# Gate logits of a windowed-attention and Sinkhorn-MoE kernel, with the attention output as the stationary operand

## The chip, the cores and the metric

The kernel runs on one core of a Trainium2 chip. The metric is the device time of the whole kernel in microseconds (us): the median over runs on the chip. One further execution of the same program was recorded by the hardware profiler, and all rows below are from that one.

## What is computed

A sliding-window attention over 2304 tokens (4 sequences of 576, 8 heads of 64), whose output `x` (2304 x 512) goes into a mixture of 8 experts. The weights of the experts come from gate logits `x @ w_gate` (2304 x 8), turned into shares by eight rounds of row and column scaling:

```python
attn = softmax(mask(scale * q @ k.T))       # window of 64, causal
x = (attn @ v).transpose(0, 2, 1, 3).reshape(B * S, H * D)

logits = x @ w_gate                          # N x 8
logits = logits - logits.max()
P = np.exp(logits)
for _ in range(8):
    P /= P.sum(1, keepdims=True) + 1e-09
    P /= P.sum(0, keepdims=True) + 1e-09
    P *= N / E
for e in range(E):
    out += P[:, e:e + 1] * (np.maximum(x @ w1[e], 0.0) @ w2[e])
```

All operands are float32.

## The kernel before, in words

The tokens are 18 tiles of 128 (`T` is 18); the 512 features are `KD` = 4 blocks of 128. The kernel has two stages.

The first, some 196 us, is the loop over `s` (line 622). Step `s` loads a later tile, makes the scores of tile `s` (`products`, matmuls on line 415), transposes the next tile's keys and queries (`transposes`, line 395), transposes the softmax of tile `s - 1` (`attn_T`, line 469) and multiplies it by the values (`values`, line 484). The result stands in PSUM with the features on the partitions and the tokens along the free dimension. ScalarE rounds it to fp32r (the type that TensorE multiplies in a single pass) into `xs[j][:, 0]` (line 490), VectorE puts the remainder into `xs[j][:, 1]` (line 491), and ScalarE copies the plain float32 into `xr[j]` (line 494). A pair of tiles shares one `j`. A product of such split operands is three matmuls: high by high, high by low, low by high.

Between these, `do_fill` takes the first half of expert 0 from a list: `mm1_s` (line 569, hidden layer of one pair of tiles, 12 matmuls of 256 columns) and `mm2_s` (line 583, output of one tile, 12 matmuls of 512 columns). Every even step from 4 on also calls `gate(j)` right after the scores, and `gate_T(j)` near its end. After the loop (lines 722 to 731) come the last gate, the rest of the list and the maximum of all logits.

`gate` multiplies in plain float32: for each feature block, the gate weights `wg` (128 x 32, of which 8 columns are used and the rest are zero) are the stationary operand and 256 columns of `xr` move (line 526). Each of the four blocks writes 32 partitions of its own in one PSUM tile. ScalarE copies that tile to `gt` (line 528). `gate_T` turns `gt` back with two transposes (line 535), and VectorE adds the four blocks into `logit` (line 536). In the profile a plain float32 matmul shows as two matmul records, so the four of a gate are `x8` there.

The second stage is the remaining seven and a half experts, three passes over six tiles each, in Strassen-like products (line 217, line 276, line 1194). It uses `logit` through `prob`, at its start.

The order on each engine is the order of the calls in the code (`tc.manual_schedule()`): each engine works through its queue in that order. PSUM tiles named `hp` and `yp` come from one pool of three buffers (line 327), handed out in turn.

Of the kernel before, what the change touches and what calls it, by code (L numbers as in the profile page):

```python
# [8 lines left out]
F32 = mybir.dt.float32  # L9
F32R = mybir.dt.float32r  # L10
AF = mybir.ActivationFunctionType
ALU = mybir.AluOpType
AX = mybir.AxisListType
# [8 lines left out]
def window_attention_sinkhorn_moe(ctx: ExitStack, tc: tile.TileContext, q, k, v, w_gate, w1, w2, out):  # L22
    nc = tc.nc
    B, H, S, D = q.shape
    NT, DM = out.shape
    E, _, FF = w1.shape
    P = 128
    WIN = 64
    T = NT // P
    KD = DM // P  # L30
# [20 lines left out]
    ident = const.tile([P, P], F32, name="ident")  # L51
    make_identity(nc, ident)
    logit = const.tile([P, T, E], F32, name="logit")
# [22 lines left out]
    def f32(ap):  # L76
        return ap.bitcast(F32)
# [126 lines left out]
    ps = {}  # L204
# [104 lines left out]
    qT, kT, s_t, r_t, nm_t, sum_t, aT, xr = {}, {}, {}, {}, {}, {}, {}, {}  # L309
# [13 lines left out]
    with tc.manual_schedule():  # L323
        with ExitStack() as p1:
            at_p = p1.enter_context(tc.tile_pool(name="at", bufs=2))
# [24 lines left out]
                    return masks["bot"]  # L350
                return masks["mid"]

            wg = at_p.tile([P, KD, 32], F32, name="wg", tag="wg", bufs=1)
            nc.vector.memset(wg, 0.0)

            def load_v(t):
                x = at_p.tile([P, H, D], F32, tag="v", name="v", bufs=3)
                for o, n, bb, s in runs(t):
                    nc.sync.dma_start(out=x[o:o + n], in_=v[bb, :, s:s + n, :].rearrange("h p d -> p h d"))
                raw["v", t] = x  # L360

            def load_kq(t, parts=((0, H),)):
                x = at_r.tile([P, 2, H, D], F32, tag="kq", name="kq")
                raw["kq", t] = x
                for h0, h1 in parts:
                    for i, src in enumerate((k, q)):
                        for o, n, bb, s in runs(t):
                            nc.sync.dma_start(out=x[o:o + n, i, h0:h1], in_=src[bb, h0:h1, s:s + n, :].rearrange("h p d -> p h d"))

            def load_vs(t):  # L370
                x = at_p.tile([P, H, D], F32, tag="vs", name="vs")
                if t == 0:
                    nc.vector.memset(x[0:WIN], 0.0)
                else:
                    nc.sync.dma_start(out=x[0:WIN], in_=raw["v", t - 1][WIN:P])
                nc.sync.dma_start(out=x[WIN:P], in_=raw["v", t][0:WIN])
                raw["vs", t] = x
# [143 lines left out]

            def gate(j):

                gp = ps["h"]()
                for kk in range(KD):
                    nc.tensor.matmul(gp[32 * kk:32 * kk + 32, :2 * P], lhsT=wg[:, kk, :], rhs=xr[j][:, kk, :], start=True, stop=True)
                gt = at_p.tile([P, 2 * P], F32, tag="gt", name="gt", bufs=1)
                nc.scalar.copy(out=gt, in_=gp[:, :2 * P])
                state_g[j] = gt

            def gate_T(j):
                gt = state_g.pop(j)
                gq = ps["h"]()[:, :2 * P].rearrange("p (t c) -> p t c", t=2)
                for i in range(2):
                    nc.tensor.transpose(gq[:, i, :], gt[:, i * P:(i + 1) * P], ident)
                nc.vector.tensor_reduce(
                    out=logit[:, 2 * j:2 * j + 2, :], in_=gq.rearrange("p t (a c) -> p t c a", a=4)[:, :, 0:E, :], axis=AX.X, op=ALU.add)

            later = []
            state_g = {}  # L540
            xs = {}


# [4 lines left out]
            def fetch_s(kind, c):  # L548
                if kind == "w1":
                    stg = r_stg.new()  # L550
                    nc.sync.dma_start(out=stg, in_=w1[0, :, c * P:(c + 2) * P].rearrange("(k p) f -> p k f", p=P))
                    return [stg[:, :, 0:P], stg[:, :, P:2 * P]]

                stg = acc[:, c:c + 2, :]
                nc.sync.dma_start(out=stg, in_=w2[0, c * P:(c + 2) * P, :].rearrange("(c p) d -> p c d", p=P))
                return [stg[:, 0, :], stg[:, 1, :]]
# [65 lines left out]
            for s in range(T + 1):  # L622
                if s + 2 < T and s != 3:
                    load_kq(s + 2)
                if s == 1:
                    held.append(fetch_s("w1", 2))
                if s < T:
                    load_vs(s)
                if s + 1 < T:
                    load_v(s + 1)  # L630
                if s == 3:
                    x_parts(0)
                if s == 0:
                    held.append(fetch_s("w1", 0))
                if s == 1:
                    nc.sync.dma_start(out=wg[:, :, 0:E], in_=w_gate.rearrange("(k p) e -> p k e", p=P))
                if s == 2:
                    held.append(fetch_s("w2", 0))
                    load_kq(5)
                    held.append(fetch_s("w2", 2))  # L640
                joint = 2 <= s < T
                ahead = s in (1, 2)
                if s < T:
                    products(s, (0, 1) if joint else (0,))
                    masked(s, 0)
                if s >= 4 and s % 2 == 0:
                    gate((s - 4) // 2)
                if s < 2:
                    keep_clock(4 if s else 0)
                if s == 3:  # L650
                    keep_clock(4, ps["h"]()[:, :P])
                    do_fill(1)
                if s + 1 < T:
                    transposes(s + 1)
                if s == 1:
                    keep_clock(2)
                if s < T and not ahead:
                    exps(s, 0)
                if joint:
                    masked(s, 1)  # L660
                if later:
                    later.pop(0)()
                if s != 3:
                    do_fill(1)
                if 0 <= s - 1 < T:
                    attn_T(s - 1, 0)
                if s < 2:
                    products(s, (1,))
                    masked(s, 1)
                if ahead:  # L670
                    if s == 2:
                        keep_clock(11, ps["h"]()[:, :P])
                    attn_T(s - 1, 1)
                    exps(s, 0)
                if s < T:
                    normalise(s, 0)
                if s == 0:
                    keep_clock(4)
                if 0 <= s - 1 < T and not ahead:
                    attn_T(s - 1, 1)  # L680
                if s > 2:
                    warm_weights(s)
                if s == 2:
                    values(1, lambda: exps(2, 1))
                elif s < T:
                    exps(s, 1)
                if later:
                    later.pop(0)()
                do_fill(1 if s < T else 0)
                if s == 3:  # L690
                    warm_weights(s)
                if s >= 4 and s % 2 == 0:
                    gate_T((s - 4) // 2)
                if s == 1:
                    keep_clock(4)
                if 0 <= s - 1 < T:
                    if s != 2:
                        values(s - 1)
                    raw.pop(("v", s - 2), None)
                if s < T:  # L700
                    normalise(s, 1)
                if s < 3:
                    warm_weights(s)
                if s >= 2 and s % 2 == 0:
                    j = s // 2 - 1
                    if j:
                        x_parts(j)
                    for c in range(4):
                        fill.append((0.5, lambda c=c, j=j: mm1_s(j, c)))
                    for t in (2 * j, 2 * j + 1):  # L710
                        fill.append((1, lambda t=t: mm2_s(t)))
                if s == T - 4:
                    fetch1(0)
                    sums1(0)
                if s == T - 3:
                    split1(0)
                    fetch1(1)
                    fetch2(0)
                if s == T - 1:
                    sums1(1)  # L720

            do_fill(0.5)
            gate(T // 2 - 1)
            do_fill(1)
            gate_T(T // 2 - 1)
            nc.vector.tensor_reduce(out=max1, in_=logit, axis=AX.XY, op=ALU.max)
            do_fill(1)
            mp = ps["h"]()[0:1, :P]
# [61 lines left out]
        with ExitStack() as p2:  # L790
# [85 lines left out]
            for u in range(n_units):  # L876
                s = 2 * u
# [98 lines left out]
        with ExitStack() as p3:  # L976
# [352 lines left out]
            for p, F, S, flow in plans:  # L1329
# [24 lines left out]
                for i in range(1, n):  # L1354
                    e = groups[i][0]
# [14 lines left out]
                a, b = S[-1][1], S[-1][0]  # L1370
# [112 lines left out]
```

## Time and profile before

| what | us |
|---|---|
| median of 3 runs | 1555.45 |
| lowest and highest run | 1554.54, 1555.67 |
| profiled execution, first to last instruction (span) | 1553.7 |
| TensorE matmul busy | 1546.4 |
| TensorE weight load busy | 1476.7 |
| VectorE busy | 965.2 |
| ScalarE busy | 761.3 |
| GpSimd busy | 990.6 |

The profiled execution has no device time of its own beside its span; the median of the runs is 1.75 us above that span, which is the launch and end around the first and last instruction. PE is the matmul part of TensorE and PEld its weight loads, which overlap the matmuls. Matmuls are pipelined, so the duration of one is longer than the distance from one to the next; what a stretch of matmuls costs is read from the chain of waits, where pieces follow each other without overlap.

### The profile page before, as it was taken

The page shows a single profiled execution, that of the slowest core. Times are in us where ns is not written, and L with a number is a line of the kernel's source. Part 1 is how long each engine was busy: PE and PEld are TensorE (multiplying, and loading weights), DVE is VectorE, ACT ScalarE, POOL GpSimd, SP SyncE. Part 2 cuts the span into 40 slices and gives each one's busy share as a digit, 9 for nine tenths or more (in the row PEclk, how much of TensorE's full clock was granted, in tenths as well). Part 3 has the DMA queues.
Part 4 walks back from the last instruction along what each step waited for, and adds up shares of the span by engine and source line. Part 5 has one row for each costly group of instructions (what it writes and reads, how often), then busy time and mean ns, then how long its engine had stood idle before and what let it go on. Part 6 is the DMA issues. An engine that isn't in the chain of part 4 may idle for free.

```text
span 1553.7 us, 27222 instructions
## 1 busy us (share of the span) xinstructions
PE 1546.4 (100%) x9703; PEld 1476.7 (95%) x9703; DVE 965.2 (62%) x1794; ACT 761.3 (49%) x1677; POOL 990.6 (64%) x925
## 2 busy tenths in 40 slices
PE   9999999999999999999999999999999999999998
PEld 8888889989998899899999999999999999999998
DVE  6766566665555555665665665665755675666666
ACT  6666535443443344355555554544554544554552
POOL 6244467668767776356677677566676566567565
PEclk9999999999999999999999999999999999999999
DMA  9876467557766766796766766655975665665643
GB/s 214 226 168 148 132 235 285 204 191 270 270 232 238 253 224 211 272 352 195 244 205 217 248 207 196 221 180 182 355 253 179 203 209 174 207 210 171 204 158 102
DMA packets 239876, 335.70 MB, mean 216 GB/s; under 512 B 71122, under 2 KB 154174, under 8 KB 235774
## 3 DMA queue, kind: packets, MB, share of 16 engines
q1 hardware_dynamic: 239742, 333.97, 66.6%
q8 instruction: 77, 1.26, 0.3%
q14 instruction: 57, 0.47, 0.1%
HBM read 236.34 MB, written 90.63 MB: 210 GB/s over the span
## 4 chain that ended last, share of the span: by engine, by line
PE 97%; DMA 1%; POOL 1%; DVE 1%; ACT 0%; SPq 0%; issue 0%; POOLq 0%; DVEq 0%; ACTq 0%
PE qb L217 18%; PE y L276 15%; PE qa L217 12%; PE qb L1194 12%; PE qc L217 12%; PE qa L1194 8%; PE qc L1194 8%; PE yp L583 3%; PE hp L569 3%; PE vp L484 1%; PE sp L415 1%; PE tp L469 1%; PE tp L395 1%; DMA acc<-in_moe_w_dram 1%; POOL w1c L164 0%; DMA kq<-in_q_dram 0%
## 5 line engine op out<-in xcount | busy, mean ns | idle before, releaser
L217 PE MATMUL qb<-xc,w1c 128*128 128x384 f32 x1620 | 321.2, 336 | 0.0
L1081 POOL TENSOR_TENSOR G<-sm,G 128x384 fp32r<-128x384 f32 x176 | 178.9, 1016 | 197.4 <-ACT G L1077 195.5
L217 PEld LDWEIGHTS qb<-xc,w1c 128*128 128x128 f32 x1620 | 284.9, 188 | 0.8 <-ACT qb L1095 0.3
L276 PE MATMUL y<-w2c,g 128*128 128x512 f32 x1080 | 251.3, 391 | 0.1
L276 PEld LDWEIGHTS y<-w2c,g 128*128 128x128 f32 x1080 | 201.8, 188 | 42.3 <-DVE acc L295 0.5
L217 PE MATMUL qa<-xc,w1c 128*128 128x384 f32 x1080 | 213.4, 337 | 0.0
L217 PE MATMUL qc<-xc,w1c 128*128 128x384 f32 x1080 | 213.0, 336 | 0.0
L217 PEld LDWEIGHTS qa<-xc,w1c 128*128 128x128 f32 x1080 | 190.4, 188 | 1.2
L217 PEld LDWEIGHTS qc<-xc,w1c 128*128 128x128 f32 x1080 | 190.1, 188 | 0.0
L1202 DVE TENSOR_TENSOR acc<-qb,acc 128x384 f32<-128x384 f32 x171 | 95.1, 556 | 123.3 <-PE qb L1194 110.7
L774 POOL TENSOR_TENSOR w2c<-wr,w2c 128x512 fp32r<-128x512 f32 x99 | 126.2, 1293 | 32.9 <-ACT w2c L773 31.6
L774 POOL TENSOR_TENSOR wp<-wr,wp 128x512 fp32r<-128x512 f32 x100 | 127.7, 1294 | 26.8 <-ACT wp L773 23.9
L178 POOL TENSOR_TENSOR w2c<-stg,w2c 128x512 fp32r<-128x512 f32 x60 | 83.8, 1417 | 93.8 <-PE qb L217 81.7
L1077 ACT CAST G<-sm 128x384 fp32r<-128x384 f32 x180 | 92.3, 514 | 64.3 <-DVE sm L1088 64.3
L1194 PE MATMUL qb<-G,w2c 128*128 128x384 f32 x552 | 111.2, 336 | 0.0
L1194 PE MATMUL qb<-G,wp 128*128 128x384 f32 x528 | 106.2, 336 | 0.0
L1194 PEld LDWEIGHTS qb<-G,w2c 128*128 128x128 f32 x552 | 97.7, 188 | 0.0
L295 DVE SCALAR_TENSOR_TENSOR acc<-y,prob,acc 128x512 f32<-128x512 f32 x72 | 54.0, 750 | 69.4 <-PE y L276 68.8
L1194 PEld LDWEIGHTS qb<-G,wp 128*128 128x128 f32 x528 | 93.4, 188 | 0.0
L1202 DVE TENSOR_TENSOR acc<-qc,acc 128x384 f32<-128x384 f32 x116 | 64.4, 555 | 41.3 <-PE qc L1194 40.6
L463 POOL TENSOR_TENSOR s<-s,rr 128x512 f32<-128x512 f32 x36 | 37.5, 1041 | 77.1 <-DVE rr L462 66.9
L162 ACT CAST w1c<-ws 128x1024 fp32r<-128x1024 f32 x30 | 31.6, 1054 | 99.4 <-POOL ws L147 99.4
(214 smaller groups left out, 2950.6 us busy)
## 6 DMA issues: line engine op xcount, KB each, us to landing
w1c<-w1d SPq DMA_DIRECT2D x300, 256.0 KB, 4.6
w1d<-w1c SPq DMA_DIRECT2D x30, 1792.0 KB, 7.8
stg<-in_moe_w_dram SPq DMA_DIRECT2D x66, 512.0 KB, 3.9
w1c<-w1d SPq DMA_DIRECT2D x60, 512.0 KB, 5.0
wr<-w2d SPq DMA_DIRECT2D x114, 256.0 KB, 3.6
wr<-in_moe_w_dram SPq DMA_DIRECT2D x85, 256.0 KB, 3.8
w2d<-tf SPq DMA_DIRECT2D x30, 512.0 KB, 4.8
vs<-v SPq DMA_DIRECT2D x35, 128.0 KB, 4.4
```

The source lines that it names most:

```text
L178: nc.gpsimd.tensor_tensor(out=w[:, 1], in0=src[:, j], in1=f32(w[:, 0]), op=ALU.subtract)
L217: nc.tensor.matmul(bank, lhsT=w[:, ws, a, kk, :], rhs=xc[xs][:, b, kk, :], start=(first and j == 0), stop=(j == 5), skip_group_check=not f ...
L276: nc.tensor.matmul(yp, lhsT=g[:, a, o:o + P], rhs=w[:, x, :], start=(i == 0), stop=(i == 11))
L295: nc.vector.scalar_tensor_tensor(out=at, in0=yp, scalar=pr, in1=at, op0=ALU.mult, op1=ALU.add)
L463: nc.gpsimd.tensor_tensor(out=st, in0=st, in1=rr[:, :, None].to_broadcast([P, 4, P]), op=ALU.mult)
L569: nc.tensor.matmul(hp, lhsT=w1s[c][:, a, kk, :], rhs=xs[j][:, b, kk, :], start=(i == 0), stop=(i == 3 * KD - 1))
L583: nc.tensor.matmul(yp, lhsT=g[:, a, o * P:(o + 1) * P], rhs=w[:, x, :], start=(i == 0), stop=(i == 11))
L774: nc.gpsimd.tensor_tensor(out=t[:, :, 1, :], in0=r, in1=f32(t[:, :, 0, :]), op=ALU.subtract)
L1077: nc.scalar.copy(out=self.g[:, k, 0, :], in_=src)
L1081: eng.tensor_tensor(out=self.g[:, k, 1, :], in0=src, in1=f32(self.g[:, k, 0, :]), op=ALU.subtract)
L1194: nc.tensor.matmul(bank, lhsT=W[p, u, wp][:, g, y, cols], rhs=G7[p, 2 * u + g][:, gp, x, :], start=(start and j == 0), stop=(j == 5), skip ...
L1202: nc.vector.tensor_tensor(out=at, in0=src, in1=at, op=ALU.add)
```

## The change

The gate's operands change places. The stationary operand is now a 128 x 128 block of `xs`, high or low part, and the moving operand is a new tile `wgs` that holds the split gate weights: for the high part of `x`, 16 columns of high and low weights, for the low part the high weights and 8 zero columns. The logits of 128 tokens come out with the tokens on the partitions, so there is no copy to `gt`, no transpose back, and one PSUM tile less per gate. VectorE adds the two halves. `wgs` is made once, at step 3, by two ScalarE casts and one GpSimd subtraction. `xr` stays: lines 503 to 512 use it.

```diff
-            wg = at_p.tile([P, KD, 32], F32, name="wg", tag="wg", bufs=1)
-            nc.vector.memset(wg, 0.0)
+            wg = at_p.tile([P, KD, E], F32, name="wg", tag="wg", bufs=1)
+            wgs = at_p.tile([P, KD, 2, 2, E], F32R, name="wgs", tag="wgs", bufs=1)
+            nc.vector.memset(f32(wgs), 0.0)
...
             def gate(j):
 
-                gp = ps["h"]()
-                for kk in range(KD):
-                    nc.tensor.matmul(gp[32 * kk:32 * kk + 32, :2 * P], lhsT=wg[:, kk, :], rhs=xr[j][:, kk, :], start=True, stop=True)
-                gt = at_p.tile([P, 2 * P], F32, tag="gt", name="gt", bufs=1)
-                nc.scalar.copy(out=gt, in_=gp[:, :2 * P])
-                state_g[j] = gt
-
-            def gate_T(j):
-                gt = state_g.pop(j)
-                gq = ps["h"]()[:, :2 * P].rearrange("p (t c) -> p t c", t=2)
+                gp = ps["h"]()[:, :4 * E].rearrange("p (t a c) -> p t a c", t=2, a=2)
                 for i in range(2):
-                    nc.tensor.transpose(gq[:, i, :], gt[:, i * P:(i + 1) * P], ident)
-                nc.vector.tensor_reduce(
-                    out=logit[:, 2 * j:2 * j + 2, :], in_=gq.rearrange("p t (a c) -> p t c a", a=4)[:, :, 0:E, :], axis=AX.X, op=ALU.add)
+                    for kk in range(KD):
+                        for a in range(2):
+                            nc.tensor.matmul(gp[:, i], lhsT=xs[j][:, a, kk, i * P:(i + 1) * P], rhs=wgs[:, kk, a], start=(kk + a == 0), stop=(kk == KD - 1 and a == 1))
+                nc.vector.tensor_reduce(out=logit[:, 2 * j:2 * j + 2, :], in_=gp.rearrange("p t a c -> p t c a"), axis=AX.X, op=ALU.add)
...
                 if s == 1:
-                    nc.sync.dma_start(out=wg[:, :, 0:E], in_=w_gate.rearrange("(k p) e -> p k e", p=P))
+                    nc.sync.dma_start(out=wg, in_=w_gate.rearrange("(k p) e -> p k e", p=P))
+                if s == 3:
+                    for a in range(2):
+                        nc.scalar.copy(out=wgs[:, :, a, 0], in_=wg)
+                    nc.gpsimd.tensor_tensor(out=wgs[:, :, 0, 1], in0=wg, in1=f32(wgs[:, :, 0, 0]), op=ALU.subtract)
...
-                if s >= 4 and s % 2 == 0:
-                    gate_T((s - 4) // 2)
...
-            gate_T(T // 2 - 1)
```

The order on TensorE in step 6, before, from the scores to the values (rows left out are the other `yp` products of the same two tiles):

```order
L415 MATMUL sp<-kT,qT 64x128 x16
L526 MATMUL hp<-xr,wg 32x256 x4
L395 MATMUL tp<-ident,kq 128x128 x8
L583 MATMUL yp<-w2c_232,g_0_991 128x512 x3
...
L535 MATMUL hp<-ident,gt 128x128 x2
L484 MATMUL vp<-aT,vs 64x64 x4
```

and in the changed kernel, where the same calls have other line numbers (415 is 416, 395 is 396, 583 is 575, 484 is 485):

```order
L416 MATMUL sp<-kT,qT 64x128 x16
L529 MATMUL hp<-wgs,xs 128x16 x16
L396 MATMUL tp<-ident,kq 128x128 x8
L575 MATMUL yp<-w2c_233,g_0_1002 128x512 x3
L575 MATMUL yp<-w2c_234,g_1_1018 128x512 x3
```

The gate keeps its place and has 16 matmuls instead of 4; the two transposes ahead of the values are gone.

The order on VectorE in the same step, before:

```order
L436 TENSOR_TENSOR s<-sp,mask_mid 128x512
L441 TENSOR_REDUCE nm<-s 128x4
L397 COPY kT<-tp 128x4x128
...
L462 RECIPROCAL rr<-rr 128x4
L536 TENSOR_REDUCE logit<-hp 128x16
L491 TENSOR_TENSOR xs<-vp,xs 128x4x128
```

and in the changed kernel:

```order
L437 TENSOR_TENSOR s<-sp,mask_mid 128x512
L442 TENSOR_REDUCE nm<-s 128x4
L530 TENSOR_REDUCE logit<-hp 128x16
L398 COPY kT<-tp 128x4x128
...
L463 RECIPROCAL rr<-rr 128x4
L492 TENSOR_TENSOR xs<-vp,xs 128x4x128
```

The sum into `logit` moves from the end of the step to a place ahead of the copy of the transposed keys.

The order on ScalarE at step 3, in the changed kernel:

```order
L553 CAST w1s_231<-stg_353 128x512
L553 CAST w1s_232<-stg_353 128x512
L631 CAST wgs<-wg 128x4x8 x2
L564 ACTIVATE g_0_648<-hp 128x256
```

The two casts of the gate weights are new there, between the casts of line 561 and the first activation of line 572 before.

## Rows read from the trace of the kernel before

**Rows 1.** The page: busy time of the engines, chain that ended last.

```profile
PE 1546.4 (100%) x9703; PEld 1476.7 (95%) x9703; DVE 965.2 (62%) x1794; ACT 761.3 (49%) x1677; POOL 990.6 (64%) x925
...
PE 97%; DMA 1%; POOL 1%; DVE 1%; ACT 0%; SPq 0%; issue 0%; POOLq 0%; DVEq 0%; ACTq 0%
```

**Rows 2.** Windows, core 0: us, busy of PE, PEld, DVE, ACT, POOL, PEclk, DMA.

```profile
54.00:160.00 106.00, 106.00 (x1303) 93.43 (x1303) 71.62 (x155) 69.81 (x195) 47.62 (x61) 1.00 0.72 169
```

**Rows 3.** Chain of waits in order of time, two steps: start us, us, what.

```profile
55.54 1.03 PE sp L415 x32
56.58 0.57 PE hp L526 x8
57.15 1.02 PE tp L395 x8
...
60.91 0.87 PE tp L469 x8
61.79 2.77 PE yp L583 x12
64.56 0.22 PE hp L535 x2
...
66.89 1.02 PE tp L395 x8
67.91 2.85 PE hp L569 x24
...
200.28 1.04 PE qa L217 x6
```

**Rows 4.** Weight loads by shape, 0 to 200 us: busy, mean ns | idle before.

```profile
L569 PEld LDWEIGHTS hp<-xs,w1s 128*128 128x128 f32 x432 | 52.5, 188 | 0.9 <-issue 0.6 <-DVE xs L491 0.3
...
L469 PEld LDWEIGHTS tp<-ident,s 128*128 128x128 f32 x144 | 16.5, 141 | 1.7 <-POOL s L463 0.4 <-issue 0.2
...
L526 PEld LDWEIGHTS hp<-xr,wg 128*32 128x32 f32 x72 | 1.4, 108 | 1.6 <-issue 1.6
...
L729 PEld LDWEIGHTS hp<-ident,max 128*1 128x1 f32 x1 | 0.1, 82 | 0.0
```

**Rows 5.** Timeline of weight loads, 195.8 to 197.3: start us, us, what [idle before].

```profile
196.23 0.29 PEld L817 LDWEIGHTS qc<-max,ones 1*128 1x128 f32 x2 [0.35 <-issue]
196.54 0.30 PEld L849 LDWEIGHTS qb<-xc 128*128 128x128 f32 x2
```

**Rows 6.** Timeline of PE after the first gate.

```profile
37.35 3.15 PE L583 MATMUL yp<-w2c,g 128*128 128x512 f32 x12
...
41.14 0.66 PE L469 MATMUL tp<-ident,s 128*128 128x128 f32 x4 [0.19 <-POOL s L463]
41.55 2.99 PE L583 MATMUL yp<-w2c,g 128*128 128x512 f32 x12
```

**Rows 7.** Chain of waits around the last two gates.

```profile
175.76 2.98 PE yp L583 x12
...
179.26 0.59 ACT aT L471
...
184.02 0.57 PE hp L526 x8
184.59 3.05 PE hp L569 x24
...
187.86 2.84 PE hp L569 x24
```

**Rows 8.** Timeline of ScalarE at step 3.

```profile
29.33 0.39 ACT L572 ACTIVATE g<-hp 128x256 fp32r<-128x256 f32 x1 [1.04 <-PE hp L569]
```

**Rows 9.** Timeline of VectorE in step 6.

```profile
64.81 0.23 DVE L536 TENSOR_REDUCE logit<-hp 128x16 f32<-128x64 f32 x1 [2.65 <-PE hp L535]
```

**Rows 10.** Timeline of PE: matmuls on a tile of ones, the first ones and later ones.

```profile
1.03 3.78 PE L617 MATMUL idle<-ones 128*128 128x128 f32 x16 [1.03 <-DVE ones L50]
...
19.78 2.62 PE L617 MATMUL hp<-ones 128*128 128x128 f32 x22
```

More of the change, by code (lines that the diff above doesn't have):

```diff
@@ L522, in gate @@
             def gate(j):
-                gp = ps["h"]()
-                for kk in range(KD):
-                    nc.tensor.matmul(gp[32 * kk:32 * kk + 32, :2 * P], lhsT=wg[:, kk, :], rhs=xr[j][:, kk, :], start=True, stop=True)
-                gt = at_p.tile([P, 2 * P], F32, tag="gt", name="gt", bufs=1)
-                nc.scalar.copy(out=gt, in_=gp[:, :2 * P])
-                state_g[j] = gt
-            def gate_T(j):
-                gt = state_g.pop(j)
-                gq = ps["h"]()[:, :2 * P].rearrange("p (t c) -> p t c", t=2)
+                gp = ps["h"]()[:, :4 * E].rearrange("p (t a c) -> p t a c", t=2, a=2)
                 for i in range(2):
-                    nc.tensor.transpose(gq[:, i, :], gt[:, i * P:(i + 1) * P], ident)
-                nc.vector.tensor_reduce(
-                    out=logit[:, 2 * j:2 * j + 2, :], in_=gq.rearrange("p t (a c) -> p t c a", a=4)[:, :, 0:E, :], axis=AX.X, op=ALU.add)
+                    for kk in range(KD):
+                        for a in range(2):
+                            nc.tensor.matmul(gp[:, i], lhsT=xs[j][:, a, kk, i * P:(i + 1) * P], rhs=wgs[:, kk, a], start=(kk + a == 0), stop=(kk == KD - 1 and a == 1))
+                nc.vector.tensor_reduce(out=logit[:, 2 * j:2 * j + 2, :], in_=gp.rearrange("p t a c -> p t c a"), axis=AX.X, op=ALU.add)
             later = []
-            state_g = {}
             xs = {}
```

## The prediction

> **What bounds the kernel now.** I read the page first: TensorE's matmul row is busy through the whole span, and the chain of work that ended last runs 97% through it [rows 1]. A kernel that is TensorE's from end to end still has stretches with other limits, so I read the stretch that the change touches. In the windows, TensorE has not one idle slice between 54 and 160 us, while VectorE, ScalarE and GpSimd are busy for 72, 70 and 48 us of those 106 [rows 2]. The chain in order of time then gives the price of each piece there: it goes from one TensorE piece to the next, with nothing of another engine between [rows 3]. So in this stage a microsecond added to TensorE's queue is a microsecond of kernel time, and a microsecond taken from another engine is worth nothing. Two places differ. After the first gate TensorE waits for GpSimd [rows 6], and around the last two gates the chain passes through ScalarE's copy of the transposed softmax [rows 7].
>
> **What the change removes.** Per gate, 0.57 us in the chain for the four matmuls on `wg` (eight records), the same at 56.58 and at 184.02 [rows 3, 7]. They are cheap for their columns because each of the four fills only 32 columns of the array and the four run side by side. The two transposes of `gate_T` cost 0.22 us [rows 3]. Eight of the nine lie in the chain. The eighth call, in the last step, lies in the wait for ScalarE's copy at 179.26 [rows 7] and saves nothing. Removed: 9 x 0.57 = 5.13 us and 8 x 0.22 = 1.76 us.
>
> ScalarE's nine copies to `gt` and VectorE's wait of 2.65 us for the transposes [rows 9] go too. Both are off the path, and I price them at nothing: the cover is TensorE itself, which waits for neither engine between 54 and 160 us [rows 2].
>
> **What it adds.** Per gate 16 matmuls (two tiles, four feature blocks, two parts), each with its own 128 x 128 stationary block in fp32r and 16 columns moving. No row of before has this form, so I bound it. Two things could set the pace: the columns that move or the weights that load.
>
> By columns: fp32r matmuls of 256, 384 and 512 columns follow each other in 2.85 / 24 = 0.119, 1.04 / 6 = 0.173 and 2.77 / 12 = 0.231 us [rows 3]. That is 0.44 ns a column, so 16 columns would take 0.119 - 240 x 0.00044 = 0.014 us, and 16 of them 0.22 us.
>
> By weights: loads of 1, 32 and 128 columns last 82, 108 and 188 ns [rows 4]. That is a fixed 82 ns, under which the next load can already run, and 106 ns that grow with the columns, 0.83 ns each. The pairs in the timeline say the same: two loads of 188 ns take 0.30 us together, so the second starts 0.11 us after the first [rows 5]. In the long products this is hidden, since a load of 0.11 us fits under a matmul of 0.119 us or more [rows 3]. With 16 columns moving there is nothing left to hide it under. I take **0.11 us** a matmul, the row nearest in kind: 16 x 0.11 = 1.76 us a gate, against 0.57. The least the loads allow is 0.106 and the most, if the 256-column pace is itself that of its loads, 0.119.
>
> Nine gates: 9 x (1.76 - 0.57) = **+10.71 us**. From this come off:
> - the transposes, **-1.76 us**;
> - the wait after the first gate. From 37.35 to 41.55 the queue takes 4.20 us for one set of 12 products and eight transposes, which elsewhere take 2.77 + 0.87 = 3.64 us [rows 3, 6]. The 0.56 us between are waits for GpSimd's weights and its softmax, and a later gate fills them: **-0.56 us**;
> - the change of array shape. Work on the full array that follows small tiles starts late: eight transposes take 1.02 us after the scores or the narrow gate, 0.87 us after full-size work [rows 3]. With a full-size gate this is paid by the gate and no longer by the transposes behind it, net zero. Only the last gate has full-size work on both sides, and there 3.05 - 2.85 = 0.20 us vanish [rows 3, 7]: **-0.20 us**.
>
> Sum: 10.71 - 1.76 - 0.56 - 0.20 = **+8.2 us**, with +7.6 at 0.106 and +9.5 at 0.119 us a matmul.
>
> The small edits go together. The two casts and the subtraction on 128 x 32 elements at step 3 are bounded by nothing below and 0.39 us each above, the row of an eight times larger activation beside them [rows 8]. ScalarE waits 1.04 us for TensorE right behind them [rows 8], and whatever reached TensorE would end in the 0.56 us counted above. The sum into `logit` now stands ahead of the copy of the keys on VectorE, 0.23 us [rows 9]. The scores of the next step need that copy, but a whole step later. One PSUM tile less per gate only loosens the rotation of three. `xs` is finished before `xr`, so the gate waits for nothing new.
>
> The profiled execution has a span of 1553.7 us and would go to 1561.9; the median of the runs stands 1.75 us above that span, so the forecast for the median is 1555.45 + 8.2 = **1563.6 us**.
>
> **Rivals.** Slower or faster here means by over 0.2% (3.1 us), about what a measurement of this kernel can tell from no change.
>
> *Columns set the pace.* If the weight loads kept ahead of the short matmuls, a gate would be 0.22 us: 9 x (0.22 - 0.57) - 1.76 - 0.20 = -5.1 us, **1550.3 us**, faster. It decides as soon as loads follow each other in under some 0.04 us. For it speaks that TensorE fetches weights ahead; against it, that even loads without a wait between them start 0.11 us apart [rows 5]. The Trainium skill, page "TensorE: Matmul & The Clock Gate", section "Back-to-back issue gap", gives about 25 ns from start to start for 1 to 64 moving columns; by that the gate would take 0.4 us and the kernel an estimated 1552.0 us, and no row of before has so few columns in a run to test it. Chance 6%.
>
> *Loads at the speed of the transposes.* The float32 transposes load 128 columns in 141 ns [rows 4], 59 above the fixed 82. If fp32r blocks taken from `xs` loaded like that, the gate would be 16 x 0.059 = 0.94 us, the first one hidden whole: 8 x 0.37 - 1.76 - 0.20 = +1.0 us, **1556.5 us**, no change that can be told. Against it: all fp32r loads of 128 columns here last 188 ns, the 432 of the hidden layer as an example [rows 4]. The Trainium skill, the page "TensorE: Matmul & The Clock Gate" again, section "Weight-path perf modes", says that a fast load turns itself on for 128 weights unless the type is FP32, at about twice the speed; by that the gate would be an estimated 0.85 us and the kernel about the time of before, and the 188 ns row says that fp32r does not get it. Chance 8%.
>
> *Load and matmul in series.* If a load could not run under so short a matmul, each pair would cost more. The one pair with a tiny moving operand, one column, takes 196.54 - 196.23 = 0.31 us for two, 0.155 each [rows 5]: 9 x (2.48 - 0.57) - 2.52 = +14.7 us, **1570.1 us**. With no overlap at all, 0.188 + 0.014 = 0.20 us, it would be +21.4 us, 1576.9 us. Against it: loads of 188 ns starting 0.11 us apart do overlap [rows 5]. Chance 14%.
>
> *The clock falls.* Its granted level is 1.00, 2.4 GHz, through the stage [rows 2], and a gate is now 1.8 us of little arithmetic between scores and transposes. At the start, where TensorE had done nothing, matmuls on ones took 3.78 / 16 = 0.236 us, later 2.62 / 22 = 0.119 us [rows 10]. If each gate brought the lower level, 1.2 GHz, for the 1.02 + 2.77 us behind it, nine gates would cost 34 us more, some **1598 us**. Against it: scores, narrow gate and transposes in a row did not lower it. Chance 4%.
>
> **How the numbers follow.** The forecast, loads in a row at 0.106 to 0.119 us, gets the remaining 68%. Faster: 6%, the columns. No change: 8%, the fast loads. Slower: 68 + 14 + 4 = 86%. The range takes the forecast, the fast loads and the lower half of the series case, 68 + 8 + 7 = 83%: **1556 to 1570 us**.
>
> **What would show it.** In the chain after, the gate should be a piece of 16 matmuls of about 1.9 us (1.76 and 0.15 for the change of shape), the transposes behind it 0.87 instead of 1.02 us, and the two steps from scores to scores 1.0 us longer. The weight loads of the gate should last 188 ns and start 0.11 us apart. PEclk should stay 1.00. A gate of under 1 us, or a wait of TensorE for another engine inside the stage, would make the prediction wrong.

## The result and the profile after

| what | before | after |
|---|---|---|
| median of 5 runs each on one chip, us | 1555.21 | 1564.93 |
| lowest and highest run, us | 1554.54, 1555.67 | 1564.61, 1565.89 |
| profiled span, us | 1553.7 | 1563.9 |
| first stage, to the first matmul of `qb<-xc`, us | 196.5 | 204.6 |
| second stage, from there to the end, us | 1357.2 | 1359.3 |

The ratio is 1.0063 with a 95% interval of 1.0052 to 1.0075: the changed kernel is slower by 9.7 us, where 8.2 were forecast. The profiled execution of the changed kernel is the slowest of its five runs (spans 1562.6 to 1563.9 us).

The page of the changed kernel: TensorE has 54 more matmul records, and the chain that ended last, 97% TensorE before [rows 1], now has 2% of GpSimd.

```profile
PE 1555.1 (99%) x9757; PEld 1489.0 (95%) x9757; DVE 964.9 (62%) x1794; ACT 758.7 (49%) x1670; POOL 991.8 (63%) x926
...
PE 94%; POOL 2%; DMA 1%; DVE 1%; ACT 1%; issue 0%; SPq 0%; POOLq 0%; DVEq 0%; ACTq 0%
```

The windows of the stretch that [rows 2] show for before: TensorE is still never idle, at a granted clock of 1.00, and the other three engines have slack as before.

```profile
54.00:162.00 108.00, 108.00 (x1312) 98.00 (x1311) 68.06 (x149) 64.93 (x184) 44.73 (x58) 1.00 0.68 159
```

The chain in order of time, at the places of [rows 3] and [rows 7]:

```profile
55.65 1.03 PE sp L416 x32
56.68 1.88 PE hp L529 x16
58.56 0.95 PE tp L396 x8
59.51 2.76 PE yp L575 x12
...
77.69 1.88 PE hp L529 x16
...
191.25 1.69 PE hp L529 x16
192.94 5.79 PE hp L561 x48
```

The gate has gone from 0.57 to 1.88 us, the piece of `gate_T` (0.22) is gone, and from one gate to the next pass 77.69 - 56.68 = 21.01 us. Before, the same period was 76.60 - 56.58 = 20.02 us, with the first of them in [rows 3] and the second here:

```profile
76.60 0.57 PE hp L526 x8
```

The weight loads, as groups by shape over the first stage, and then the timeline of one gate:

```profile
L561 PEld LDWEIGHTS hp<-xs,w1s 128*128 128x128 f32 x432 | 52.4, 188 | 0.4 <-DVE xs L492 0.3 <-issue 0.2
L529 PEld LDWEIGHTS hp<-wgs,xs 128*128 128x128 f32 x144 | 16.8, 191 | 1.4 <-issue 1.2
```

```profile
56.61 1.86 PEld L529 LDWEIGHTS hp<-wgs,xs 128*128 128x128 f32 x16 [0.17 <-issue]
```

Sixteen loads of 0.19 us each take 1.86 us from the first start to the last end, so they start (1.86 - 0.19) / 15 = 0.111 us apart.

After the first gate, the timeline of TensorE no longer shows the waits of [rows 6]; from one set of products to the next pass 41.88 - 38.25 = 3.63 us, where it was 4.20:

```profile
38.25 3.00 PE L575 MATMUL yp<-w2c,g 128*128 128x512 f32 x12
41.09 1.04 PE L470 MATMUL tp<-ident,s 128*128 128x128 f32 x8
41.88 1.39 PE L575 MATMUL yp<-w2c,g 128*128 128x512 f32 x5
```

So far this is the prediction: the first stage is 8.0 us longer (204.56 against 196.54). Some 2 us of the profiled execution are in the second stage, which the change does not touch. There the waits of TensorE between 190 and 560 us, none before, now have one line:

```profile
PE qb L217 <- ACT qb L237: 1.6, 2, 1.4
```

I followed it back through the changed kernel. ScalarE's timeline:

```profile
365.61 1.04 ACT L162 CAST w1c<-ws 128x1024 fp32r<-128x1024 f32 x1 [8.43 <-POOL ws L147]
366.56 0.47 ACT L237 COPY qb<-qa 128x384 f32<-128x384 f32 x1
```

GpSimd's timeline:

```profile
349.00 0.74 POOL L302 TENSOR_TENSOR xt<-tf 128x256 f32<-128x256 f32 x1 [8.16 <-DVE g L227]
...
364.78 0.80 POOL L147 TENSOR_TENSOR ws<-stg,ws 128x256 f32<-128x256 f32 x1
```

The timeline of SP's queue:

```profile
338.86 0.34 SPq L855 DMA_DIRECT2D tf<-xd_f  x1
```

Read from the bottom: SP issues a load of `xd_f` (activations of a later pass) at 338.86, GpSimd uses it at 349.00, 10.14 us later. (The view puts GpSimd's wait down to VectorE's `g`, which ended last, at 348.98; the load itself landed 10.0 us after its issue, so it was late by itself. In the second profile of this kernel, below, the wait is put down to the load.) Behind it GpSimd's queue holds the weight sums up to line 147, ScalarE's cast waits for them until 365.61, and the copy on line 237, for which TensorE waits, stands behind that cast. In the kernel before, the same load was used 338.76 - 330.88 = 7.88 us after its issue, and the copy waited for TensorE and not the other way round. SP's queue, before:

```profile
330.88 0.33 SPq L862 DMA_DIRECT2D tf<-xd_f  x1
```

GpSimd, before:

```profile
338.76 0.78 POOL L302 TENSOR_TENSOR xt<-tf 128x256 f32<-128x256 f32 x1 [5.90 <-DMA tf<-xd_f]
```

ScalarE, before:

```profile
355.20 1.05 ACT L162 CAST w1c<-ws 128x1024 fp32r<-128x1024 f32 x1 [8.44 <-POOL ws L147]
356.74 0.46 ACT L237 COPY qb<-qa 128x384 f32<-128x384 f32 x1 [0.48 <-PE qa L217]
```

The experiments ask two things: what makes a gate 1.88 us, and where the second stage's time comes from.

### The profile page after: what moved, and what is told of

Same layout as the page of the kernel before. It is cut to its first block, busy times and chain, and to the rows that moved or that the text cites. A ratio compares the mean times of both kernels' runs of the same rounds, so it can differ in the third digit from the quotient of the medians.

```text
span 1563.9 us, 27327 instructions
## 1 busy us (share of the span) xinstructions
PE 1555.1 (99%) x9757; PEld 1489.0 (95%) x9757; DVE 964.9 (62%) x1794; ACT 758.7 (49%) x1670; POOL 991.8 (63%) x926
## 3 DMA queue, kind: packets, MB, share of 16 engines
q8 instruction: 77, 1.26, 0.4%
## 4 chain that ended last, share of the span: by engine, by line
PE 94%; POOL 2%; DMA 1%; DVE 1%; ACT 1%; issue 0%; SPq 0%; POOLq 0%; DVEq 0%; ACTq 0%
PE qb L217 17%; PE y L276 13%; PE qb L1187 12%; PE qa L217 12%; PE qc L217 12%; PE qa L1187 8%; PE qc L1187 8%; PE hp L561 3%; PE yp L575 3%; PE vp L485 1%; PE hp L529 1%; PE sp L416 1%; PE tp L470 1%; POOL w1c L164 1%; PE tp L396 1%; DMA tf<-xd_f 1%
```

## Experiments on the gate

**128 columns moving (cols128).** The changed kernel with 112 columns of zeros beside the 16.

```diff
-            wgs = at_p.tile([P, KD, 2, 2, E], F32R, name="wgs", tag="wgs", bufs=1)
+            wgs = at_p.tile([P, KD, 2, 16, E], F32R, name="wgs", tag="wgs", bufs=1)
...
```

> The changed kernel with 128 columns moving in each gate matmul instead of 16 (the 112 more are zeros); everything else the same. If the weight load sets the pace, a gate stays at 16 matmuls in 1.88 us in the chain, starts 0.107 us apart, and the first stage ends (first matmul of line 842 before the second stage) within 0.3 us of the changed kernel's 204.6 us. If the moving columns set the pace, at 0.44 ns a column, each matmul grows by 0.049 us, a gate by 0.79 us to 2.7 us, and the stage ends near 211.7 us.

Measured: one run of 1564.4 us, and in the chain

```profile
56.66 1.93 PE hp L529 x16
58.59 0.89 PE tp L396 x8
```

Eight times the columns add 0.05 us to a gate of 16 matmuls, and the transposes behind it take 0.06 less. The columns do not set the pace.

**Half the stationary block (half_load).** The changed kernel with 64 instead of 128 tokens in each stationary block; it leaves out the logits of the other 64.

```diff
-                            nc.tensor.matmul(gp[:, i], lhsT=xs[j][:, a, kk, i * P:(i + 1) * P], rhs=wgs[:, kk, a], start=(kk + a == 0), stop=(kk == KD - 1 and a == 1))
+                            nc.tensor.matmul(gp[0:64, i], lhsT=xs[j][:, a, kk, i * P:i * P + 64], rhs=wgs[:, kk, a], start=(kk + a == 0), stop=(kk == KD - 1 and a == 1))
...
```

> The changed kernel with 64 instead of 128 columns in each gate's stationary operand: the gate logits of the first 64 tokens of each tile only, the other half of the logits left at zero. The number of matmuls, 16 a gate with 16 columns moving, stays. If the weight load sets the pace (0.83 ns a stationary column), loads last 135 ns, starts are 0.053 to 0.06 us apart, a gate takes about 1.0 us and the stage ends some 7 to 8 us before 204.6. If a fixed cost of each matmul or of accumulating into the same PSUM words sets it, a gate stays at 1.88 us and the stage ends at 204.6.

Measured: one run of 1559.86 us. The group of the gate's loads by shape:

```profile
L530 PEld LDWEIGHTS hp<-wgs,xs 128*64 128x64 f32 x144 | 9.1, 138 | 1.4 <-issue 1.2
```

The gate in the chain:

```profile
56.09 1.03 PE hp L530 x16
57.12 0.95 PE tp L397 x8
```

Half the weights take 0.85 us off a gate: 0.85 / 16 = 0.053 us a matmul, half of 0.111. The first stage ends at 197.2 us, 7.4 before that of the changed kernel. A cost that each matmul has whatever its weights would have left the gate at 1.88 us. With cols128 this settles it: the gate costs what its weights take to load.

**Each gate matmul behind a long one (interleave).** If the loads set the pace, could they hide under the 512-column products, as those of the long products do? `gate` only notes its 16 matmuls, and `mm2_s` issues one behind each product.

```diff
...
+                gate_mm(0)
...
+                        if whole or i <= 8:
+                            gate_mm(1)
...
```

> The changed kernel with the 16 gate matmuls not in a row but each behind one of the 512-column products of the same step (8 per tile, in the last two gates up to 12 and a rest in a row). If TensorE can load weights several matmuls ahead, a 512-column matmul of 0.231 us covers both loads, a gate matmul costs only its columns, 0.014 us, a gate 0.22 us, and the stage ends some 11 us before 204.6, near 193, which is ahead of the kernel before (196.6). If only one load can stand ready, the load of the gate matmul is covered but that of the long matmul behind it is not: the pair takes 0.231 + 0.107 + 0.014, a gate matmul still costs about 0.12 us, and the stage ends within 1 us of 204.6.

Measured: median 1568.34 us, ratio to before 1.0086 (1.0072 to 1.0100); the first stage ends at 207.0 us, later than with the gate in one piece. The timeline of TensorE's matmuls:

```profile
58.05 0.17 PE L539 MATMUL hp<-wgs,xs 128*128 128x16 f32 x1
58.07 0.47 PE L589 MATMUL yp<-w2c,g 128*128 128x512 f32 x1
58.38 0.17 PE L539 MATMUL hp<-wgs,xs 128*128 128x16 f32 x1
58.41 0.48 PE L589 MATMUL yp<-w2c,g 128*128 128x512 f32 x1
```

The timeline of its weight loads:

```profile
58.16 0.19 PEld L539 LDWEIGHTS hp<-wgs,xs 128*128 128x128 f32 x1
58.39 0.19 PEld L589 LDWEIGHTS yp<-w2c,g 128*128 128x128 f32 x1
58.49 0.19 PEld L539 LDWEIGHTS hp<-wgs,xs 128*128 128x128 f32 x1
```

A pair takes 58.41 - 58.07 = 0.34 us, the 0.231 of a 512-column product and 0.11 more. The gate's load (58.16) does lie under the long product. But the load for the next long product starts at 58.39, just after the short matmul has started (58.38), and not earlier, and so it goes on for the whole tile: no second load stood ready. So the 0.11 us are paid by the product behind instead. A matmul too short to cover a load costs one load in either place. The stage ends another 2.4 us later than with the gate in one piece. Of these, 1.5 us stand in the view of waits as waits that the changed kernel does not have there: 0.7 us for loads of `q` and `k`, and 0.8 us at the end of the stage for a copy of `ys` on VectorE. The rest is open.

## Experiments on the second stage

The first idea was that a first stage of other length shifts the transfers against each other; the second, that the number of TensorE's records matters. Two kernels add time to the first stage of the kernel before, by matmuls on `ones` behind each narrow gate, without the new gate.

**Four matmuls a gate, 72 records (ballast).**

```diff
+                wp = ps["h"]()[:, :P]
+                for _ in range(4):
+                    nc.tensor.matmul(wp, lhsT=ones, rhs=ones, start=True, stop=True)
```

> The kernel before with four plain float32 matmuls on a tile of ones behind each narrow gate, 0.9 to 1.05 us of TensorE time each, nothing else changed: the first stage should end 7 to 9 us later, near 204.5. The second stage takes 1357.1 us from its first matmul of line 849 to the end in the kernel before, 1359.3 us in the changed kernel. If the extra 1.7 to 2.2 us come from the first stage's end being shifted against the transfers, it takes 1358.5 to 1359.5 here too and the median is near 1565. If they come from something the change itself does, it stays at 1357.1 and the median is near 1563.5. If they are scatter of transfers from run to run, the spans of the runs here and of the kernel before scatter by about 1 us each way and neither holds cleanly.

Measured: median 1562.98 us, ratio 1.0053 (1.0040 to 1.0066). The first stage ends at 204.5 us, as in the changed kernel, and the second takes 1356.9 us with no wait on line 237. A first stage longer by 8 us does not by itself lengthen the second.

**Three matmuls a gate, 54 records (ballast54).** The same with `range(3)`, as many records as the change adds.

> The kernel before with three plain float32 matmuls on ones behind each narrow gate instead of four, so 54 more matmul records in the first stage, exactly as many as the changed kernel has (the first ballast had 72 more). The theory of code fetches: the instruction transfers of TensorE come every so many instructions, and with 54 more of them one falls into the burst of transfers near the start of the fifth round of the second stage; the first load of xd_f then takes about 10 us from its issue to its first use instead of 7.8, TensorE waits for ScalarE's copy (line 237) there, and the second stage, from the first matmul of line 849 to the end, takes 1358 to 1360.5 us. The first stage should end near 202.6, the median be near 1562.5. The rival, that the changed kernel's own instructions or tiles cost that time, leaves the second stage at 1356.8 to 1357.4, no wait at line 237, the median near 1560.7.

Measured: median 1563.26 us, ratio 1.0055 (1.0042 to 1.0067), no less than with four matmuls, though the first stage ends 2.5 us earlier, at 202.0. The second takes 1359.8 us, the `xd_f` load is used 10.4 us after its issue, and the wait is there:

```profile
PE qb L217 <- ACT qb L237: 2.2, 2, 1.6
```

So the second stage's loss comes without the new gate.

**The changed kernel with 18 more records (after72).** One such matmul behind each gate, 72 more records than before in all.

> The changed kernel with one plain float32 matmul on ones behind each gate: 18 more matmul records, 72 more than before in all, as in the first ballast, about 0.24 us a gate. First stage to end near 206.8. If the place of TensorE's code fetches makes the difference, the first load of xd_f is used 7.8 us after its issue, there is no wait at line 237 and the second stage takes 1356.8 to 1357.4 us: median near 1565, although 2.1 us of work are added to a kernel of 1564.9. If the change itself costs that time, the second stage stays at 1357.8 to 1360.5 and the median is near 1567.

Measured: in the profile as the count would have it (second stage 1356.9 us, load used after 8.0 us, no wait), but the median is 1566.66 us (1565.75 to 1568.11), and the profiled execution is the fastest of its runs. The median lies nearer the 1567 of the rival than the 1565 of the count, so this run supports the count in one execution only; what the slower ones spent is open.

**Both kernels once more (before_again, after_again).** Is the loss the kernel's or one execution's?

> The kernel before, once more, for a second profile: if the second stage's length hangs on where things fall in the program and not on the run, it takes 1356.8 to 1357.4 us from the first matmul of line 849 to the end again, with 7.7 to 8.0 us from the issue of the first load of xd_f to its first use. If it is scatter from run to run, it can come out 1 to 2 us longer.

> The changed kernel, unchanged, profiled once more. Theory (the number of TensorE's records sets where the q8 transfer falls beside the first xd_f load, so the delay belongs to the kernel and not to one run): the first stage ends at 204.4 to 204.8 us, the first xd_f load is used about 10 us after its issue, TensorE waits at line 237 for 0.7 to 2.0 us, the second stage takes 1358 to 1359.5 us. Rival (the delay is one run's chance): the load is used 7.8 to 8.0 us after its issue, no wait at line 237, the second stage takes 1356.8 to 1357.2 us.

Measured: before_again 1554.71 us, second stage 1357.0, load used after 7.96 us, no wait. after_again 1565.36 us (1554.22 for the one run of the kernel before on the same chip), second stage 1358.8, load used after 10.31 us, and

```profile
PE qb L217 <- ACT qb L237: 1.5, 1, 1.5
```

The loss came again in the second profile of the changed kernel and stayed away in the second of the kernel before: it belongs to the kernel and not to one execution.

**GpSimd's sums on the load put behind its weight sums (late_sums).** The decisive one: the load may be as late as it likes, but nothing that TensorE needs soon stands behind it.

```diff
-                x_sums(side["xt"][:, :, :, j * P:(j + 1) * P], x, nc.gpsimd)
+                side["late"] = lambda: x_sums(side["xt"][:, :, :, j * P:(j + 1) * P], x, nc.gpsimd)
...
                         sums1(s + 2)
+                        if "late" in side:
+                            side.pop("late")()
```

> The changed kernel with GpSimd's four sums on an xd_f load put behind its four weight sums of the next group (lines 144 to 147), so that GpSimd no longer stands at the late load; same work, same transfers, same TensorE records as in the changed kernel. Theory (the second stage's extra 2 us come from the late first xd_f load through GpSimd, ACT's copies and the wait of TensorE at line 237): the first stage ends at 204.4 to 204.8 us, the load may still land late, but TensorE does not wait at line 237 and the second stage takes 1356.8 to 1357.4 us; median near 1563.2 (span 1561.3 + 2.0). Rival (the late load is only a sign of something else, or the delay is made by another transfer): the wait stays and the second stage takes 1358.5 to 1359.5 us, median near 1565.

Measured: median 1563.45 us (1563.27 to 1563.80), ratio to before 1.0055 (1.0041 to 1.0069). The first stage ends at 204.67, the second takes 1356.8 us, and TensorE waits for nobody between 190 and 560 us. GpSimd's timeline:

```profile
343.30 0.74 POOL L147 TENSOR_TENSOR ws<-stg,ws 128x256 f32<-128x256 f32 x1
349.26 0.74 POOL L302 TENSOR_TENSOR xt<-tf 128x256 f32<-128x256 f32 x1 [5.22 <-DMA tf<-xd_f]
...
361.97 0.80 POOL L147 TENSOR_TENSOR ws<-stg,ws 128x256 f32<-128x256 f32 x1
```

ScalarE's timeline has the copy on line 237 waiting for TensorE again:

```profile
364.81 0.46 ACT L237 COPY qb<-qa 128x384 f32<-128x384 f32 x1 [0.96 <-PE qa L217]
```

The load, issued at 339.00, is still used only 10.26 us later, but the first weight sums are done ahead of it, and the next ones, for which ScalarE's cast waits, end at 362.8 instead of 365.6 us. The second stage is 2.5 us shorter than in the profile of the changed kernel, as short as before. The median is 1.5 us lower; against the kernel before on the same chip, 8.9 us are left of 9.7, so 0.8 us by that measure (the medians of before differ by 0.7 in the two comparisons). All five spans, 1561.2 to 1561.8 us, lie under all five of the changed kernel. The chain from the late load through GpSimd and ScalarE to TensorE is shown.

Why the load is late is shown only as a coincidence, which holds in all 14 profiles, those of the next section too. The DMA view names a queue q8, "instruction", with 77 packets of 1.26 MB in all. Its place against the first `xd_f` issue (where the half-microsecond window that has it begins), with the rest:

| kernel | PE records | second stage, us | load used after, us | q8 packet from the issue, us |
|---|---|---|---|---|
| before, before_again | 9703 | 1357.2, 1357.0 | 7.88, 7.96 | +9 |
| ballast, after72 | 9775 | 1356.9, 1356.9 | 7.75, 8.00 | -4 |
| after, after_again | 9757 | 1359.3, 1358.8 | 10.14, 10.31 | 0, -0.5 |
| cols128, half_load | 9757 | 1357.9, 1360.6 | 9.62, 10.51 | +0.5, +1 |
| interleave, ballast54 | 9757 | 1358.6, 1359.8 | 10.24, 10.40 | -0.5, +0.5 |
| late_sums | 9757 | 1356.8 | 10.26 | -0.5 |
| pack_turns | 9691 | 1359.3 | 8.19 | +11.5 |
| pack_turns12, pack12_again | 9703 | 1358.6, 1359.3 | 8.02, 8.42 | +9, +9.5 |

With 54 more records a q8 packet goes out within one and a half microseconds of the load's issue, and the load is used after 9.6 to 10.5 us; in all others the packet is 3.5 us away or more, and the load is used after 7.8 to 8.4. One window of the DMA view of the changed kernel, 338 to 339 us, has both:

```profile
q8 instruction: 1, 0.02, 11.8%
issues: line engine op xcount, KB each, median us to landing
tf<-xd_f SPq DMA_DIRECT2D x1, 512.0 KB, 10.0
```

The packet's place follows the number of TensorE's instructions (a record is a matmul, and each has a weight load): against the kernel before, 24 fewer bring it 2.5 us later, 108 more 8 to 9.5 us earlier and 144 more 13 us earlier, 0.07 to 0.10 us an instruction. That fits code which is fetched in order. That q8 carries TensorE's code, and that its packet is what delays the load, is argued from this and not shown. No run takes the packet away by itself.

## A version meant to beat both

**Four gates turned back at once (pack_turns).** If 16 loads are dear and the narrow gate cheap, the gain must come from `gate_T`. The gates keep the shape of before, but gate `j` writes its logits into rows `8 * (j % 4)` of each block of 32 (weights `wg4`), VectorE adds four gates into one `gt`, and two transposes turn four gates back.

```diff
+                r = j % 4
...
-                    nc.tensor.matmul(gp[32 * kk:32 * kk + 32, :2 * P], lhsT=wg[:, kk, :], rhs=xr[j][:, kk, :], start=True, stop=True)
+                    nc.tensor.matmul(gp[32 * kk:32 * kk + 32, :2 * P], lhsT=wg4[:, kk, r].rearrange("p a c -> p (a c)"), rhs=xr[j][:, kk, :], start=True, stop=True)
...
+                    nc.vector.tensor_tensor(out=gt, in0=gp[:, :2 * P], in1=gt, op=ALU.add)
...
+                if j % 4 != 3 and j != T // 2 - 1:
+                    return
...
```

> The kernel before with the narrow gates kept and the turning back done for four gates at once: the gate weights of gate j stand in the columns 8 (j mod 4) of a strip of 32, so that four gates fill the strips of one SBUF tile (VectorE adds each to it), and two transposes turn four gates. 6 transposes instead of 18, of which 2 instead of 8 calls in the chain: 6 x 0.22 = 1.3 us off the first stage, which ends near 195.3. It has 12 matmul records fewer, so the second stage may come out at 1357 or, if a code fetch falls badly, up to 2 us longer; the median lies between 1553.3 and 1555.5. A gain would put this version ahead of both kernels.

Measured: 1555.40 us over 11 runs, ratio 1.0002 (0.9993 to 1.0011). The first stage ends at 194.8 us, 1.7 earlier, and the second takes 1359.3 us, with waits on line 237 of 0.9 us, although the load is used after 8.19 us. This execution is the slowest of the 11, but the median too shows no gain: what the first stage gains the second loses.

**The same with the records of before (pack_turns12).** Twelve records fewer than before might be the reason, so six matmuls of one column put them back at places where TensorE waits.

```diff
+            def blanks(n, dst):
+                for _ in range(n):
+                    nc.tensor.matmul(dst, lhsT=ones, rhs=ones[:, 0:1], start=True, stop=True)
...
```

> pack_turns with 6 fp32 matmuls of one column added at places where TensorE waits anyway (12 records), so that TensorE has as many records as the kernel before, while the gates keep the shape of pack_turns. Theory (the first stage gains from fewer transposes, and the second stage is longer or shorter by where the transfers of the q8 queue, which I take for TensorE's instruction fetches, fall among the data loads): first stage ends at 194.8 to 195.5 us as in pack_turns, the second stage takes 1356.8 to 1357.4 us as in the kernel before, with no wait of TensorE at line 237, the first xd_f load is used 7.8 to 8.0 us after its issue; median near 1553.2, about 0.1% under the kernel before. Rival (pack_turns' own edits, its tiles and adds, make the second stage longer, whatever the number of records): the second stage stays at 1358 to 1359.5 us, with waits at line 237, median near 1555.4, no difference to the kernel before.

> pack_turns12, unchanged, profiled once more. If the VectorE operation of 1.71 us at line 227, after which its second stage fell behind in the first profile, was that run's chance, the second stage takes 1356.8 to 1357.6 us here; if it belongs to the kernel's placing of GpSimd and VectorE, it takes 1358 to 1359 us again, with a VectorE operation of over 1.5 us at line 227 near 585 us. In both cases the first xd_f load is used about 8 us after its issue and TensorE does not wait at line 237.

Measured: 1555.43 us over 11 runs, ratio 1.0005 (0.9996 to 1.0014). The theory fell on the time and held on the load: it is used 8.02 us after its issue with q8 9 us away, TensorE does not wait at line 237, and still the second stage takes 1358.6 us. The profile has another place of loss, VectorE's timeline near 585 us:

```profile
584.90 1.71 DVE L227 SCALAR_TENSOR_TENSOR g<-u,g 128x384 fp32r<-128x384 f32 x1 [0.59 <-ACT g L222]
```

The same operation takes 0.60 us in before_again. The second profile (1556.05 us) has it again:

```profile
585.29 1.70 DVE L227 SCALAR_TENSOR_TENSOR g<-u,g 128x384 fp32r<-128x384 f32 x1 [0.59 <-ACT g L222]
```

In both, the products on line 276 behind it fall back by another 0.8 to 0.9 us against the profile of before_again. In the second profile the load is used after 8.42 us, and TensorE waits 0.6 us at line 237, where none was expected. So pack_turns has places of loss of its own, which the count of records does not decide. No kernel of these runs is faster than the one before: both versions stand 0.5 to 0.8 us above it in the medians, which can't be told from no change.

## Why the prediction was right

**Loads in a row, 0.11 us a matmul: right.** Measured 0.111. A gate takes 1.88 us where 1.91 were forecast (1.76 and 0.15 for the change of shape). half_load and cols128 show that it is the loads. The Trainium skill, page "TensorE: Matmul & The Clock Gate", section "Back-to-back issue gap", gives about 25 ns for 1 to 64 moving columns, and says of its formula for a matmul by itself that at small sizes it leaves out the weight load. Here 16 columns with new weights each go at 111 ns, so the 25 ns, which one rival took for such a run, do not hold where every matmul brings its own weights. The section "Weight-path perf modes" of that page has the fast load turn itself on for 128 weights unless the type is FP32, and does not name fp32r. The loads of the gate take 191 ns each, against 188 for the other fp32r blocks: none of them was fast.

**Transposes -1.76 and the wait after the first gate -0.56: right.** Both pieces are gone, and from gate to gate 0.99 us are added, where 1.91 - 0.57 - 0.15 - 0.22 = 0.97 were forecast.

**The change of shape: roughly right.** The transposes behind the gate take 0.95 us, neither 1.02 nor the forecast 0.87. The last gate, with full-size work on both sides, takes 1.69 us (1.76 forecast) and the 48 matmuls behind it 5.79 us (5.89 before, 5.69 forecast); together 7.48 us, where 7.45 were forecast.

**The first stage: right.** +8.0 us for the forecast +8.2. The casts and the moved sum cost nothing that the chain shows, and the granted clock stayed at 1.00. After the start of the stage (from 40 us on) the view of waits has TensorE wait for another engine once, 0.3 us for ScalarE's copy of the transposed softmax. The prediction took a wait inside the stage as a sign of being wrong; this one is the wait in which the eighth call of `gate_T` lay before, where the prediction said that nothing is saved, and it adds nothing.

**The step that was off** is the sentence that the change stays in its stage: the forecast added +8.2 to the whole span and priced everything behind at nothing. The second stage lost 1.8 to 2.1 us in the two profiles and, by what late_sums gives back, 0.8 to 1.5 in the medians. Before, TensorE had no such wait, but the trace shows how near it was: the copy on line 237 waited only 0.48 us for TensorE, with GpSimd's chain right ahead of it. That row was there to be read, and the prediction did not look at it.

A smaller error is the time around the span, 1.75 us in the forecast. It is 2.0 in the runs of the changed kernel (1564.93 and a span of 1562.9) and 1.7 in those of before, which adds 0.3. The same 2.0 stands in all kernels with the new gate, and 1.7 in both ballasts, so it comes with the change; I have no cause for it. Together: 8.0 + 0.3 and 0.8 to 1.5 are 9.1 to 9.8 us, against 9.7 measured.

**The rivals.** Columns: fell with cols128. Fast loads: the 191 ns. Series: would have made 16 x 0.155 = 2.48 us a gate. The clock: stayed at 1.00 in the stage.

## What to carry to other kernels

Where TensorE bounds a stage, price a matmul by the longer of its columns and its weight load: with a new fp32r block of 128 x 128 for every matmul, fewer than some 250 columns (0.111 us at 0.44 ns a column) are hardly cheaper, and the load isn't hidden by a long product beside it. So put the operand with the fewer changes of weights in the stationary place, even if the result then has to be turned back: two transposes (0.22 us) cost far less than going from 0.57 to 1.88 us a gate. And when a change moves nothing behind it, still look in the later stages for chains that end just before TensorE needs them: half a microsecond of slack there can go when a transfer comes two microseconds later.

## What I had not expected of the hardware

- In interleave only one weight load stood ready: the load for the long product did not start under the product before it, and the pair took 0.34 us instead of 0.23.
- A load of 512 KB on the same queue, issued behind the same transfers, is used after 9.6 to 10.5 us in all kernels with 9757 TensorE records and after 7.8 to 8.4 us in those with 9691, 9703 or 9775: 54 matmul records in the first stage were enough to move it. What makes it late is argued, not shown.
- A VectorE operation that takes 0.60 us in before_again took 1.7 us in both profiles of pack_turns12, at the same point of the program. What held it was not tried.
